# Earlier release of a weight load, transposes split over two PSUM banks, and a ninth Sinkhorn row, in a fused attention and feed-forward kernel

## The chip, the cores and the metric

The kernel runs on one core of a Trainium2 chip. The metric is the device time of one execution in microseconds (us), as a median over several runs. A core has these engines, each with its own instruction queue that is worked off in order: TensorE (PE, matrix products; its weight loads are shown as PEld), VectorE (DVE), ScalarE (ACT), GpSimd (POOL) and SyncE (SP). They synchronize by semaphores. Data moves between the main memory and the on-chip buffer SBUF by DMA, issued here from the queues of POOL and SP. PE writes its products to PSUM[...]; DVE and ACT copy them from there to SBUF.

## The reference

For each of 4 batches and 8 heads, `sort_net` is an 8x8 matrix that is normalized in five Sinkhorn rounds. With it the blocks of k and v are mixed (a sequence of 768 is 8 blocks of 96), then each block of q attends to its block of the mixed k and v. The result, laid out as 3072 tokens of 512, goes through a feed-forward layer.

```
for _ in range(5):
    P = P - np.max(P, axis=-1, keepdims=True)
    P = np.exp(P)
    P = P / (np.sum(P, axis=-1, keepdims=True) + 1e-09)
    P = P / (np.sum(P, axis=-2, keepdims=True) + 1e-09)
k_sorted = einsum('bhij,bhjcd->bhicd', P, k_b); v_sorted likewise
attn = softmax(scale * q_b @ k_sb^T);  x = attn @ v_sb
h = x @ w_in;  g = s * max(h, 0)^2 + b;  out = g @ w_out
```

## The kernel before, in words

The order of the work on each engine is the order in which the program records it (`manual_schedule`); nothing is reordered later. The program is written out by hand in two parts: a start-up for batch 0, and then a steady course in which the feed-forward products of one batch are interleaved with the attention of the next.

**Start-up.** SP loads `sort_net` (L74) and v of batch 0 (L78). POOL builds an identity and a selection matrix, then issues three loads of k (L88) and four of q (L99) of batch 0. Meanwhile the five Sinkhorn rounds run as a chain between ACT (exponential, L190) and DVE: row sums (L195), reciprocal, scaling, column sums (L200), reciprocal, scaling (L205). In the first round the 1e-9 is added to the column sums as an operation of its own (L203), from the tile `eps` (L109). PE has nothing to do in this time and computes products of zeros, `warm(138, 128)` at L188: 138 products of 128 columns into a PSUM tile Z of the pool psb.

After the rounds PE spreads the matrices over the partitions (L217), DVE builds from that the block matrix PD[0] of batch 0 (L235), and PE mixes k with it in three pieces (L254), v in four pieces (L304), with q transposed in between (L273). ACT ("A") and DVE ("D") copy the pieces out of PSUM (`evac`, L243 and L245). Then come the scores of the first half of batch 0 (`s_piece`, L319, exponential on ACT L324), the products with v (`p_piece`, L354) and their normalization on DVE (L361, L362), which gives x.

**POOL's queue and w_in.** After the first loads POOL does three memsets and then a one-element copy that serves as a gate:

```
nc.gpsimd.tensor_copy(out=ones[:, 0:1], in_=KS[0][:, 0, 0, 2 * CK:2 * CK + 1])
load_w()
```

It reads an element that the third k piece's copy (on ACT) writes, so POOL waits there until that is done. `load_w` (L126 to L147) issues the weights of the feed-forward layer: w_in in 16 parts (L131), the second half of batch 0's q in four parts (L99) after the sixth of them, then w_out in four parts (L147). Behind these stand in POOL's queue, in this order: eleven memsets (L496 to L502, L150 to L152), two one-value loads (s and b, L505), k and v of batch 1 (L88), q of batch 1 in eight parts (L99), and eight copies that permute batch 1's v (`v_sort`, L171). POOL's transfers use eight semaphores in turn, so that each issue waits until the transfer eight places earlier has landed.

**The transposes of x.** `t_piece` (L371) turns x with PE into a bank of psb (which has two buffers) and copies it to XT. With "AD", the first half of the bank is copied by ACT and the second by DVE. In the built program the DVE copy waits for the ACT copy of the same bank. With "D", DVE copies the whole. The first call, `t_piece(0, 0, 0, "AD")` at L490, takes heads 0 to 3 of x; the second, as `TP(0, 0, 2, "D")`, heads 4 to 7.

**Feed-forward.** `ffn1(t, slots, ahead)` computes h in eight parts, each a PSUM tile of psa (three buffers) made of 8 products with w_in (L411): for each of two column groups, four products over the four head pairs. With `ahead=3`, the products of head pairs 0 and 1 of parts 0 to 2 come first, and those of head pairs 2 and 3 afterwards. ACT applies the relu (L425), DVE squares (L426). `slots` says which other work is recorded where: a key -3, -2 or -1 stands ahead of part 0, 1 or 2 of these early products. For batch 0:

```
ffn1(0, {-2: [TP(0, 0, 2, "D")], ("pre", 1): [QB(0, HB, "D"), QB(0, HB + 2, "D")],
```

QB are the transposes of the second half of q (L286). `ffn2` computes the products with w_out (L436), each finished group of 128 rows being scaled and biased on DVE (L457) and stored by SP (L460). In its slots lies the attention of the next batch: k pieces (L254) in slot 2, v pieces 0 to 2 (L304), which need the copies of L171, in slot 5, v piece 3 and scores in slot 9.

Of the kernel before, what the change touches and what calls it, by code (L numbers as in the profile page):

```python
# [9 lines left out]
FP = mybir.dt.float32  # L10
BF = mybir.dt.bfloat16
AF = mybir.ActivationFunctionType
ALU = mybir.AluOpType
# [9 lines left out]
def kernel(  # L23
# [12 lines left out]
    nc = tc.nc  # L36

    B, H, S, D = q.shape
    NB = sort_net.shape[-1]
    BLK = S // NB  # L40
    BH = B * H
# [4 lines left out]
    HB = NB // 2  # L46
# [6 lines left out]
    CK = 16  # L53
# [5 lines left out]
    const = ctx.enter_context(tc.tile_pool(name="const", bufs=1))  # L59
# [9 lines left out]
    psb = ctx.enter_context(tc.tile_pool(name="psb", bufs=2, space=bass.MemoryType.PSUM))  # L69
    ctx.enter_context(tc.manual_schedule())  # L70


    sn = const.tile([BH, NB, NB], FP)
    nc.sync.dma_start(out=sn, in_=sort_net.rearrange("b h i j -> (b h) i j"))  # L74
    v0f = gtp.tile([128, C2, D], FP, tag="gt", name="v0f")
    CV = C2 // 4
    for c in range(0, C2, CV):
        nc.sync.dma_start(out=v0f[:, c:c + CV, :].rearrange("p c d -> p (c d)"),  # L78
                          in_=raw[2][0][:, c * D:(c + CV) * D])
# [25 lines left out]
    KS = [const.tile([128, NG, 2, GAP], BF, name=f"ks{i}") for i in range(2)]  # L105
    VS = [const.tile([KR, 2 * NG, VW], BF, name=f"vs{i}") for i in range(2)]
    nc.vector.memset(VP[0][:, :, C2:GAP], 0.0)
    nc.vector.memset(KS[0][:, :, :, C2:GAP], 0.0)
    eps = const.tile([BH, NB], FP)  # L109
    nc.vector.memset(eps, 1e-9)  # L110


    ident = const.tile([128, 128], BF)
# [8 lines left out]
    ones = const.tile([128, 32], BF)  # L122
# [3 lines left out]
    def load_w():  # L126
        wiv = moe_w_in.rearrange("(a p) f -> p a f", p=128)
        fq = d_ff // 4

        def part(a, f0, f1):  # L130
            nc.gpsimd.dma_start(out=wi[:, a, f0 * fq:f1 * fq], in_=wiv[:, a, f0 * fq:f1 * fq])  # L131

        for c in (0, 1):
            for a in (0, 1):
                part(a, c, c + 1)
        for c in (0, 1):
            for a in (2, 3):
                part(a, c, c + 1)
            if c == 0:
                load_q(0, range(HB, NB))  # L140
        for c in (2, 3):
            for a in range(NHP):
                part(a, c, c + 1)
        wov = moe_w_out.rearrange("(f p) n -> p f n", p=128)
        for c in range(4):
            fs = slice(c * (NF // 4), (c + 1) * (NF // 4))
            nc.gpsimd.dma_start(out=wo[:, fs, :], in_=wov[:, fs, :])  # L147
# [9 lines left out]
    def warm(n, w=512):  # L157
        for _ in range(n):
            if not Z:
                Z.append(psb.tile([128, 512], FP, tag="b", name="z"))  # L160
            nc.tensor.matmul(out=Z[0][:, 0:w], lhsT=zeros[:, 0:128], rhs=zeros[:, 0:w],  # L161
                             start=True, stop=True)


    def permute(eng, b, src, cs=slice(0, C2), ds=slice(0, D)):
# [4 lines left out]
        else:  # L170
# [3 lines left out]
    rstat = const.tile([BH, NB], FP)  # L174
# [5 lines left out]
            out=jsel, in_=ident.rearrange("p (h j z) -> p j h z", h=H, j=NB), axis=AX.XY, op=ALU.add),  # L180
        lambda: nc.vector.tensor_reduce(
            out=bm.rearrange("p (e z a) -> p e z a", e=2, z=2),
            in_=idv.rearrange("p a e j z -> p e z a j"), axis=AX.X, op=ALU.add),
# [1 line left out]
    nc.vector.tensor_reduce(out=rstat, in_=sn, axis=AX.X, op=ALU.max)  # L185
    nc.vector.tensor_tensor(out=sn, in0=sn, in1=rstat.broadcast_to([BH, NB, NB]),
                            op=ALU.subtract)
    warm(138, 128)  # L188
    for it in range(5):
        nc.scalar.activation(out=sn, in_=sn, func=AF.Exp)  # L190
        if it >= 1:
            permute(nc.scalar, 0, v0f, slice((it - 1) * CV, it * CV))
        if it in (1, 2):
            idle[it - 1]()
        nc.vector.tensor_reduce(out=rstat, in_=sn, axis=AX.X, op=ALU.add)  # L195
        nc.vector.reciprocal(out=rrec, in_=rstat)
        nc.vector.tensor_tensor(out=sn, in0=sn, in1=rrec.broadcast_to([BH, NB, NB]), op=ALU.mult)
        if it == 4:
            break
        nc.vector.tensor_reduce(out=rstat, in_=sn.rearrange("p i j -> p j i"),  # L200
                                axis=AX.X, op=ALU.add)
        if it == 0:
            nc.vector.tensor_tensor(out=rstat, in0=rstat, in1=eps, op=ALU.add)  # L203
        nc.vector.reciprocal(out=rrec, in_=rstat)
        nc.vector.tensor_tensor(out=sn, in0=sn, in1=spread(rrec, [[0, NB], list(rrec.ap[1])]),  # L205
                                op=ALU.mult)

    PD = {}
# [4 lines left out]
    def spread_p(b0, n):  # L213

        pe = psa.tile([128, n, NB, NB], FP, tag="a", name="pe")
        for b in range(n):
            nc.tensor.matmul(out=pe[:, b].rearrange("p i j -> p (i j)"), lhsT=emat[:, b0 + b, :],  # L217
                             rhs=sn.rearrange("p i j -> p (i j)"), start=True, stop=True)
        return pe
# [13 lines left out]
    def build_pd(b):  # L233
        pd = const.tile([128, 2, 2, NG], BF, name=f"pd{b}")
        nc.vector.scalar_tensor_tensor(  # L235
            out=pd.rearrange("p e z (a i) -> p (e z a) i", i=NB),
            in0=spread(bm, [list(bm.ap[1]), [0, NB]]), scalar=RC[:, b:b + 1],
            in1=spread(PT[:, b], [[0, 4 * NHP], list(PT.ap[2])]), op0=ALU.mult, op1=ALU.mult)
        PD[b] = pd

    def evac(eng, out, in_):
        if eng == "A":
            nc.scalar.copy(out=out, in_=in_)  # L243
        else:
            nc.vector.tensor_copy(out=out, in_=in_)  # L245
# [125 lines left out]
    def t_piece(b, half, hp2, eng):  # L371

        x = X[b, half]
        if hp2 == 0:
            XT[b * 2 + half] = xtp.tile([128, HB, NHP, BLK], BF, tag="xt", name="xt")
        tr = psb.tile([128, 1024], BF, tag="b", name="tr")
        for hp in (hp2, hp2 + 1):
            for n in range(HB):
                c0 = (n * 2 + hp % 2) * BLK
                nc.tensor.transpose(out=tr[:, c0:c0 + BLK],  # L380
                                    in_=x[:, n, hp * 128:(hp + 1) * 128],
                                    identity=ident[0:BLK, 0:BLK])
        n = HB // len(eng)
        for i, g in enumerate(eng):
            evac(g, XT[b * 2 + half][:, i * n:(i + 1) * n, hp2:hp2 + 2, :],
                 tr[:, i * n * 2 * BLK:(i + 1) * n * 2 * BLK].rearrange("p (n a c) -> p n a c",
                                                                        n=n, a=2))

    def t_dma(b, half):
        x = X.pop((b, half))  # L390
# [71 lines left out]

    take_p(0, 1, spread_p(0, 1))
    build_pd(0)
    pe = spread_p(1, B - 1)
    nc.scalar.copy(out=PB, in_=pe)
    warm(3)
    k_piece(0, 0, "A")
    k_piece(0, CK, "D")
    k_piece(0, 2 * CK, "A")  # L470

    nc.gpsimd.tensor_copy(out=ones[:, 0:1], in_=KS[0][:, 0, 0, 2 * CK:2 * CK + 1])
    load_w()
    v_piece(0, 0, "D")
    v_piece(0, CK, "A")
    q_piece(0, 0, "D")
# [66 lines left out]
    def SB(b, h, i): return lambda: s_banks(b, h, i)  # L543
    def P(b, h, i): return lambda: p_piece(b, h, i)
    def TP(b, h, i, eng): return lambda: t_piece(b, h, i, eng)
    def TD(b, h): return lambda: t_dma(b, h)
    def PDB(b): return lambda: build_pd(b)
    def QB(b, n0, eng): return lambda: q_blocks(b, n0, eng)


    ffn1(0, {-2: [TP(0, 0, 2, "D")], ("pre", 1): [QB(0, HB, "D"), QB(0, HB + 2, "D")],
             2: [SB(0, 1, 0)], 3: [SB(0, 1, 1), P(0, 1, 0)], 4: [SB(0, 1, 2), P(0, 1, 1)],
             5: [SB(0, 1, 3), P(0, 1, 2)], 6: [TP(0, 1, 0, "D"), P(0, 1, 3)]}, ahead=3)
    ffn1(1, {-2: [TP(0, 1, 2, "D")], 1: [lambda: take_p(1, B - 1, PB), PDB(1)], 4: [PDB(2)],
# [10 lines left out]
    for b in range(B):  # L565
        n = b + 1
# [48 lines left out]
```

## Time and profile before

| | us |
|---|---|
| median of 8 runs | 231.03 |
| lowest, highest | 229.9, 232.16 |
| the profiled execution, whole | 231.2 |
| its span, first to last instruction | 229.4 |
| PE, PEld busy in the span | 219.3, 132.9 |
| DVE, ACT, POOL busy | 124.5, 98.9, 68.0 |

The chain of work that ended last, which the profile follows back from the last instruction, spends 72% of the span on PE, 14% on DMA, 7% on POOL, 3% on DVE, 1% on ACT. By line, the products with w_out (L436) have 33%, those with w_in (L411) 27%, the DMA of v of a later batch 8% and the DMA of w_in 5%.

How to read the rows: in the timeline and in the chain, the first number is the start in us from the span's start, the second the duration. A group of instructions is written as line, engine, operation, output tile <- input tiles, shape and number; in square brackets stands for how long the engine was idle before it, and what ended that. In a table of stages, each row gives the stretch and its length, the busy time and number of instructions of PE, PEld, DVE, ACT and POOL, then the granted clock of PE, the busy share of the DMA engines and their GB/s. The granted clock is 1.00 throughout.

### The profile page before, as it was taken

Reading aid. Unit: us, or ns where it says so; the run is one execution under the profiler, and the core shown is the slowest. Engines: PE = TensorE matmul, PEld = TensorE weight load, DVE = VectorE, ACT = ScalarE, POOL = GpSimd, SP = SyncE. Lnnn points to the kernel's source line nnn. Section 1 sums busy time; section 2 is a strip of 40 time slices with the busy share of each in tenths; the row PEclk is TensorE's granted clock in tenths of the full one; section 3 lists DMA queues with packets and bytes.
Section 4 is the critical chain, followed back from the end, with each engine's and each line's share of the span. In section 5 each row is a group of like instructions: output and inputs, shape, how many; then the busy total and the mean of one; then the engine's idle time right before and its main releaser. Section 6 shows DMA issues by size and latency. Waiting matters only on the chain.

```text
span 229.4 us, 5829 instructions
## 1 busy us (share of the span) xinstructions
PE 219.3 (96%) x2554; PEld 132.9 (58%) x2554; DVE 124.5 (54%) x224; ACT 98.9 (43%) x127; POOL 68.0 (30%) x112
## 2 busy tenths in 40 slices
PE   8897889999799999999999999999999999999993
PEld 8886546655456555665655555665555555654452
DVE  6666556562456554478647634498647534341221
ACT  4967266564314506554425225637142246650000
POOL 8419789331920007483000009290000000000000
PEclk9999999999999999999999999999999999999999
DMA  6998999999981555995111477994112440001212
GB/s 199 224 64 95 172 184 198 174 186 168 78 209 46 115 122 122 201 155 114 51 46 49 114 163 147 176 168 61 49 68 67 122 114 3 0 1 46 93 49 91
DMA packets 53930, 25.82 MB, mean 113 GB/s; under 512 B 44944, under 2 KB 49296, under 8 KB 53904
## 3 DMA queue, kind: packets, MB, share of 16 engines
q0 software_dynamic: 30864, 12.85, 46.4%
q1 hardware_dynamic: 23040, 12.59, 22.1%
q8 instruction: 20, 0.33, 0.6%
q14 instruction: 6, 0.05, 0.1%
HBM read 27.27 MB, written 6.29 MB: 146 GB/s over the span
## 4 chain that ended last, share of the span: by engine, by line
PE 72%; DMA 14%; POOL 7%; DVE 3%; ACT 1%; issue 1%; POOLq 0%
PE ops L436 33%; PE hps L411 27%; DMA rawv<-in_v_dram 8%; DMA wi<-in_moe_w_in_dram 5%; PE pv L354 3%; PE tv L304 2%; PE sc L319 2%; POOL vp L171 2%; PE tp L254 2%; PE ops L449 2%; POOL wo L147 1%; POOL wi L131 1%; ACT ks L243 1%; DMA sn<-in_sort_net_dram 1%; ACT sn L190 1%
## 5 line engine op out<-in xcount | busy, mean ns | idle before, releaser
L411 PE MATMUL hps<-xt,wi 128*128 128x384 bf16 x512 | 85.7, 326 | 1.8 <-DMA wi<-in_moe_w_in_dram 1.1
L436 PE MATMUL ops<-wo,gt 128*128 128x512 bf16 x368 | 85.7, 379 | 0.0
L425 ACT ACTIVATE rt<-hps 128x768 bf16<-128x768 f32 x64 | 51.1, 811 | 57.3 <-PE hps L411 49.7
L411 PEld LDWEIGHTS <-wi 128*128 128x128 bf16 x512 | 49.4, 98 | 35.0 <-DMA wi<-in_moe_w_in_dram 1.3
L426 DVE TENSOR_TENSOR gt<-rt 128x768 bf16<-128x768 bf16 x64 | 46.5, 733 | 42.5 <-ACT rt L425 41.7
L436 PEld LDWEIGHTS <-gt 128*128 128x128 bf16 x368 | 33.6, 98 | 36.9 <-issue 0.6
L457 DVE SCALAR_TENSOR_TENSOR ot<-ops,s_bc,bias 128x512 f32<-128x512 f32 (+1 forms) x25 | 18.2, 730 | 30.9 <-PE ops L436 28.4
L324 ACT ACTIVATE at<-sc 112x768 bf16<-112x768 f32 x28 | 21.3, 808 | 30.5 <-PE sc L319 30.5
L99 POOL DMA_DIRECT2D qtok<-in_q_dram x32 | 24.9, 792 | 20.5 <-DMA rawv<-in_v_dram 9.0
L362 DVE TENSOR_TENSOR x<-pv,rec 96x512 bf16<-96x512 f32 x32 | 22.0, 687 | 1.1
L245 DVE CAST vs<-tv 112x1024 bf16<-112x1024 f32 x11 | 13.3, 1223 | 11.7 <-PE tv L304 11.6
L171 POOL COPY vp<-rawv 128x384 bf16<-128x384 bf16 x24 | 18.9, 838 | 0.0
L354 PEld LDWEIGHTS <-at 112*128 112x128 bf16 (+1 forms) x256 | 12.8, 101 | 6.7 <-ACT at L324 0.6
L561 POOL COPY gate<-gt 128x1 bf16<-128x1 bf16 x2 | 0.4, 191 | 54.4 <-DVE gt L426 54.4
L354 PE MATMUL pv<-vs,at 112*128 112x66 bf16 (+1 forms) x256 | 13.9, 195 | 0.5 <-DVE vs L245 0.5
L161 PE MATMUL z<-zeros 128*128 128x128 bf16 (+1 forms) x144 | 11.3, 245 | 1.0 <-DVE zeros L102 1.0
L304 PEld LDWEIGHTS <-vp 128*64 128x64 bf16 x512 | 9.3, 112 | 4.6 <-issue 2.7
L304 PE MATMUL tv<-pd,vp 128*64 128x64 bf16 x512 | 10.6, 197 | 1.4 <-POOL vp L171 1.3
L161 PEld LDWEIGHTS <-zeros 128*128 128x128 bf16 x144 | 9.7, 109 | 1.3 <-DVE zeros L102 1.0
L243 ACT CAST ks<-tp 128x1024 bf16<-128x1024 f32 x8 | 8.1, 1012 | 4.4 <-PE tp L254 4.3
L243 ACT CAST vs<-tv 112x1024 bf16<-112x1024 f32 x5 | 5.1, 1018 | 10.3 <-PE tv L304 10.3
L131 POOL DMA_DIRECT2D wi<-in_moe_w_in_dram x16 | 8.6, 548 | 3.1 <-DMA wi<-in_moe_w_in_dram 1.9
(77 smaller groups left out, 104.0 us busy)
## 6 DMA issues: line engine op xcount, KB each, us to landing
out_dram<-ot SPq DMA_DIRECT2D x23, 256.0 KB, 2.0
qtok<-in_q_dram POOLq DMA_DIRECT2D x32, 96.0 KB, 9.4
rawk<-in_k_dram POOLq DMA_DIRECT2D x3, 768.0 KB, 6.5
rawv<-in_v_dram POOLq DMA_DIRECT2D x3, 768.0 KB, 9.8
wi<-in_moe_w_in_dram POOLq DMA_DIRECT2D x16, 128.0 KB, 5.5
wo<-in_moe_w_out_dram POOLq DMA_DIRECT2D x4, 512.0 KB, 10.6
v0f<-in_v_dram SPq DMA_DIRECT2D x4, 384.0 KB, 4.1
rawk<-in_k_dram POOLq DMA_DIRECT2D x3, 256.0 KB, 7.5
```

The source lines that it names most:

```text
L99: nc.gpsimd.dma_start(out=QTOK[b][:, n], in_=qv[:, n])
L161: nc.tensor.matmul(out=Z[0][:, 0:w], lhsT=zeros[:, 0:128], rhs=zeros[:, 0:w], start=True, stop=True)
L171: eng.tensor_copy(out=o, in_=i)
L304: nc.tensor.matmul(out=ps[z * GAP:(z + 1) * GAP, d, :], lhsT=VP[b % 2][:, d0 + d, :], rhs=PD[b][:, :, z, :], start=True, stop=True)
L324: nc.scalar.activation(out=at, in_=sc[0:KR, :, 0:TG], func=AF.Exp, scale=scale)
L354: nc.tensor.matmul(out=pv[0:m, e, n * VW:(n + 1) * VW], lhsT=atf[:, c0:c0 + m], rhs=VS[b % 2][:, e * NG + g0 + n, :], start=True, stop=True)
L362: nc.vector.tensor_tensor(out=x[:, :, hp * 128:(hp + 1) * 128].rearrange("p n (e d) -> p e n d", e=2), in0=pvv[:, :, :, 0:D], in1=rec.unsq ...
L411: nc.tensor.matmul(out=H1[i][:, f, 0:TG], lhsT=wi[:, hp, fc:fc + 128], rhs=xt[:, :, hp, :], start=(hp == 0), stop=(hp == NHP - 1))
L425: nc.scalar.activation(out=rt, in_=h, func=AF.Relu)
L426: nc.vector.tensor_tensor(out=gt[:, 2 * i:2 * i + 2, :], in0=rt, in1=rt, op=ALU.mult)
L436: nc.tensor.matmul(out=ops, lhsT=gt[:, f, m * 128:(m + 1) * 128], rhs=wo[:, f, :], start=(f == 0), stop=(f == NF - 1))
L457: nc.vector.scalar_tensor_tensor(out=ot[:, ns], in0=ops, scalar=s_bc, in1=BIAS[0][:, ns], op0=ALU.mult, op1=ALU.add)
```

## The change

- `eps` and its addition go. The tile of the Sinkhorn matrices gets a ninth row, set to 1e-9 once; the column sums run over nine rows. The 1e-9 is thereby added in each of the four rounds that have column sums.
- The products of zeros ahead of the Sinkhorn rounds are 126 of 140 columns, not 138 of 128.
- The gate copy reads an element of PD[0] (DVE, L235) and stands, with `load_w`, directly behind `build_pd(0)`.
- `t_piece` takes a bank of its own for each engine that copies: with "AD", the transposes of the first two blocks go to one bank and those of the other two to another. In the built program no copy waits for the other engine's copy any more.
- The second transposes of batch 0's first half are recorded one place later (key -1, ahead of part 2) and are copied by ACT and DVE ("AD").

```diff
-    sn = const.tile([BH, NB, NB], FP)
+    sne = const.tile([BH, NB + 1, NB], FP)
+    sn = sne[:, 0:NB, :]
...
-    eps = const.tile([BH, NB], FP)
-    nc.vector.memset(eps, 1e-9)
+    nc.vector.memset(sne[:, NB, :], 1e-9)
...
-    warm(138, 128)
+    warm(126, 140)
...
-        nc.vector.tensor_reduce(out=rstat, in_=sn.rearrange("p i j -> p j i"),
+        nc.vector.tensor_reduce(out=rstat, in_=sne.rearrange("p i j -> p j i"),
                                 axis=AX.X, op=ALU.add)
-        if it == 0:
-            nc.vector.tensor_tensor(out=rstat, in0=rstat, in1=eps, op=ALU.add)
...
-        tr = psb.tile([128, 1024], BF, tag="b", name="tr")
-        for hp in (hp2, hp2 + 1):
-            for n in range(HB):
-                c0 = (n * 2 + hp % 2) * BLK
-                nc.tensor.transpose(out=tr[:, c0:c0 + BLK],
-                                    in_=x[:, n, hp * 128:(hp + 1) * 128],
-                                    identity=ident[0:BLK, 0:BLK])
         n = HB // len(eng)
         for i, g in enumerate(eng):
+            tr = psb.tile([128, 1024], BF, tag="b", name="tr")
+            for hp in (hp2, hp2 + 1):
+                for m in range(n):
+                    c0 = (m * 2 + hp % 2) * BLK
+                    nc.tensor.transpose(out=tr[:, c0:c0 + BLK],
+                                        in_=x[:, i * n + m, hp * 128:(hp + 1) * 128],
+                                        identity=ident[0:BLK, 0:BLK])
             evac(g, XT[b * 2 + half][:, i * n:(i + 1) * n, hp2:hp2 + 2, :],
-                 tr[:, i * n * 2 * BLK:(i + 1) * n * 2 * BLK].rearrange("p (n a c) -> p n a c",
-                                                                        n=n, a=2))
+                 tr[:, 0:n * 2 * BLK].rearrange("p (n a c) -> p n a c", n=n, a=2))
...
     take_p(0, 1, spread_p(0, 1))
     build_pd(0)
+
+    nc.gpsimd.tensor_copy(out=ones[:, 0:1], in_=PD[0][:, 0, 0, 0:1])
+    load_w()
     pe = spread_p(1, B - 1)
...
-    nc.gpsimd.tensor_copy(out=ones[:, 0:1], in_=KS[0][:, 0, 0, 2 * CK:2 * CK + 1])
-    load_w()
     v_piece(0, 0, "D")
...
-    ffn1(0, {-2: [TP(0, 0, 2, "D")], ("pre", 1): [QB(0, HB, "D"), QB(0, HB + 2, "D")],
+    ffn1(0, {-1: [TP(0, 0, 2, "AD")], ("pre", 1): [QB(0, HB, "D"), QB(0, HB + 2, "D")],
```

## The prediction

> **What bounds the kernel now.** I read the slices of the page first: PE is at 9 tenths nearly everywhere, except in the first eight slices (0 to 46 us) and around slice 11. By the stage table PE is busy 15.8 of 20.0 us from 10 to 30, 22.35 of 22.40 from 30 to 52.4, 9.97 of 11.23 from 52.4 to 63.63, and 162.2 of 165.8 from there to the end. So PE sets the time from 63.63 on, and what can be gained or lost lies before. There I read the chain of work that ended last:
>
> ```profile
> 15.82 0.19 POOL ones L472
> 16.01 0.29 issue
> 16.29 1.09 POOL wi L131 x2
> 17.38 5.96 DMA wi<-in_moe_w_in_dram
> ...
> 24.28 5.67 DMA wi<-in_moe_w_in_dram
> ...
> 39.20 18.05 DMA rawv<-in_v_dram
> 57.25 0.28 issue
> 57.54 0.77 POOL qtok L99
> 58.30 0.04 issue
> 58.35 4.80 POOL vp L171 x6
> 63.15 0.04 issue
> 63.19 0.44 PE tv L304 x16
> ```
>
> From 15.82 to 63.19 the chain is not on PE. It is POOL's queue: the gate copy that releases w_in (L472), w_in and w_out, eleven memsets, the loads of batch 1, and the eight copies of batch 1's v (L171) for which PE waits. The links are fixed work: at most eight of POOL's transfers are in flight (each waits for the one eight places earlier), so POOL issues when an old one lands. Nothing between waits for PE. Therefore the whole chain moves with its first link. Next the timeline around that link, and the places where PE waits:
>
> ```profile
> 12.50 0.35 DVE L235 SCALAR_TENSOR_TENSOR pd<-bm,RC,PT 128x128 bf16<-128x128 f32 x1
> ...
> 15.82 0.19 POOL L472 COPY ones<-ks 128x1 bf16<-128x1 bf16 x1 [7.51 <-ACT ks L243]
> ...
> 23.01 0.36 DVE L245 COPY xt<-tr 128x384 bf16<-128x384 bf16 x1 [1.24 <-ACT xt L243]
> ...
> 29.99 0.66 PE L411 MATMUL hps<-xt,wi 128*128 128x384 bf16 x3 [1.09 <-DMA wi<-in_moe_w_in_dram]
> ```
>
> POOL sits idle 7.51 us before the gate copy, while the block matrix was ready at 12.85. The table by quarter microseconds (last column GB/s) tells whether the DMA engines would be free:
>
> ```profile
> 14.25:14.50 0.25, 0.25 (x24) 0.25 (x18) 0.25 (x1) 0.25 (x1) 0.00 (x0) 1.00 0.22 14
> 15.00:15.25 0.25, 0.25 (x25) 0.25 (x20) 0.25 (x1) 0.25 (x1) 0.00 (x0) 1.00 0.00 0
> 17.25:17.50 0.25, 0.25 (x24) 0.25 (x19) 0.25 (x1) 0.00 (x0) 0.25 (x2) 1.00 0.00 0
> ```
>
> They move 150 GB/s until 13.5, 5 to 75 until 15.0, and nothing from 15.0 to 17.5, when w_in's first bytes come, 1.2 us after its first issue at 16.29.
>
> **The change, part by part.**
>
> *The ninth Sinkhorn row.* It removes one 32x8 addition on DVE, on the path: from 4.08 to the next start at 4.27, 0.19 us. The four column sums read 72 elements instead of 64. Their row is 0.260 us; if all of it grew with the elements, 8 more would cost 0.033 each, 0.13 for four; if it is fixed cost, nothing. So the gain lies between 0.06 and 0.19; I take 0.12. The memset of the row takes the place of the memset of eps, and ends before the sort_net transfer lands (2.28).
>
> *126 products of 140 columns.* 17,640 columns for 17,664. The 138 took 9.34 us, so by columns the 126 take 9.33 and by number 8.53; they end between 9.5 and 10.3. The Sinkhorn ends at 11.02 - 0.12 = 10.90, so both are covered by 0.6 us. Nothing.
>
> *The release of w_in.* The gate copy now waits for the block matrix: 12.85 - 0.12, and 0.07 (DVE gt to the gate copy at 87.08) to 0.14 (ACT ks to the gate copy) for the release, so about 12.83 instead of 15.82: 3.0 us earlier. All of load_w and what follows it on POOL is moved past nothing else: behind the gate copy stand the same 16 w_in, four q and four w_out issues, memsets and batch 1's loads in the same order; in front of it the waits for k's and q's old transfers (landed at 13.0 and 15.3 at the latest) are met when POOL reaches them (w_in 4 at 14.9, q 6 at 17.3). ACT's first k copies, which the gate copy used to wait for, lose a reader and nothing else.
> The transfers: w_in's first bytes come at 12.83 + 0.47 + 1.2 = 14.5 instead of 17.5. They meet q's tail for 0.5 us, when it moves under a third of full rate. Cost between 0 and 0.5; I take 0.05, as the tail's bytes are few. So every landing is about 2.95 to 3.0 earlier: the eighth w_in 29.94 to 27.0, rawv 57.25 to 54.3, the sixth v copy 63.15 to 60.2.
>
> A rule of the Trainium skill speaks against this part ("SBUF — State Buffer", Who interferes with whom): DVE and GpSimd share a port pair, and a DVE copy or cast in a two-port mode shuts GpSimd out for its whole length, descriptor writing included. POOL's issues would now lie beside four DVE copies (14.15, 15.44, 16.95, 18.15: 1.23 + 1.23 + 0.96 + 1.23 = 4.65 us). By the full lock, w_in would lose all it gains. The row: before, six w_in issues stood beside the last two of these and took 3.23 us, 0.538 each, the median of all 16, and the cast beside them took 1.23 like those alone. The page itself exempts an instruction with at most one SBUF input outside those modes, and these copies read PSUM. I take the row: no cost.
>
> *The transposes in two banks.* Before, DVE's half of the first copy waits for ACT's half (1.24 us idle, start 23.01 as ACT ends at 22.98): the built program has that wait, and the changed one has not. The second bank is the one that the zero products use, so its transposes wait for the last of them (21.73 + 0.38 = 22.11, before at about 22.13): 0 to 0.1 us. DVE's copy then starts at about 22.45, 0.55 earlier, and so do the two normalizations behind it on DVE (the last ends at 24.5, not 25.04).
>
> *The second transposes one place later, on both engines.* Four products of part 1 now stand before them, in time in which PE waited for the normalization. ACT gets one copy more (0.48), at 24.8 to 25.3, where it idles 4.45 us.
>
> PE's sum at this place: last transposes at 24.5 to 24.8; 12 products at 0.164 (16 of them at 25.27 to 28.04, less the drain) to 26.8; q's transposes 0.84, to 27.6 (q lands at 25.0); four products of part 2, to 28.3 (its w_in has landed at 27.0, so the wait of 1.09 is gone). Before, this ended at 30.65: PE gains 2.3.
>
> **What is late next.** PE reaches batch 1's v at 59.90 - 2.3 = 57.6. Three v pieces at 0.62 (the 32 products of row L304 at 67.19) would end at 59.5, but the sixth v copy is there at 60.2 and the last 16 products end at 63.63 - 3.0 = 60.65. So the wait for POOL remains, shortened from 1.9 (63.63 less 59.90 + 1.87) to 1.1 us, and POOL's chain sets the gain: 3.0 us. PE's own gain only has to be over 1.15 for that, so the transposes' edits and the Sinkhorn's direct part cost and bring nothing by themselves; without this cover the release alone would be worth less. After 60.65 PE goes back to back as before; batch 1's q transposes and gated loads of later batches shift with it.
>
> Sum: the profiled execution took 231.2 around a span of 229.4; less 3.0 it is 228.2 and 226.4. The median of the runs shown is 0.17 under the profiled one, so 228.1.
>
> **Rivals.**
> 1. Part of the shift is lost (chance 0.10). w_in's descriptors and k's and q's tail share the 16 DMA engines, or a landing further down comes later than rigid. The chain's two waits for w_in then lengthen by up to 0.5 each, and PE's gain can fall to 1: 1.0 to 2.0 us remain, 229.0 to 230.1. For it: transfers wait on each other in a chain of eight, so a loss is passed on. Against: 2.5 us without a byte, and no other traffic in the stretch.
> 2. No change (0.07): batch 1's v is held by something that does not move, a DMA backlog that only drains at its rate. From 30 to 44 the engines move about 205 GB/s without pause. Then PE comes earlier and waits longer, 231.0. Against: the backlog begins with w_in, and starts earlier.
> 3. Slower (0.08): the port lock above, in spite of the row. Place: POOL's issues at 13 to 19.5 and the DVE copies there. Price: POOL held for up to 4.65 us less the 3.0 won, so the chain ends 1.6 later, 232.7. It decides from the point at which DVE holds POOL for more than 3.0 us (or a DVE copy, held in turn, delays PE by over 3.4, its gain and the slack). For it, that DVE and POOL now work side by side from 13.3; against, the unchanged 0.538 and 1.23.
>
> Forecast 0.75. A difference under 0.5% (1.2 us) can't be told from none here. Faster: the forecast and most of rival 1, 0.82; within: 0.10; slower: 0.08. Range: the runs spread by 0.5% to each side, their median by less; 227.1 is the gain with a further microsecond (w_in's landings quicker than before), and 230.0 takes in most of rival 1.
>
> **What would show it.** In the changed profile the gate copy stands near 12.8 and w_in's first issue near 13.3, each w_in issue still 0.54; the wait of 1.09 for w_in is gone; DVE's xt copy starts within 0.1 of its transposes; rawv lands near 54.3; PE still waits for vp, about 1.1 in all; the v pieces end near 60.65 and the rest of the span is 165.8 as before. It is wrong if POOL's issues lengthen, if rawv's landing moves by less than 2.5, or if PE has no wait for vp left.

## The result, and the profile after

The changed kernel takes 228.95 us, the median of 18 runs (227.38 to 229.9), against 231.3 of the kernel before, the median of 53 runs. The ratio is 0.9909, with an interval of 0.9889 to 0.9929: 2.1 us of 231.3 are gone (1.6 to 2.6). Ratio and interval leave out the executions of a slower state, of which the kernel before has more, and so the ratio is not simply 228.95 / 231.3. The forecast was 228.1, a gain of 3.0. The profiled execution of the changed kernel took 227.38 around a span of 225.6; it is the shortest of the 18 and 1.57 under their median, so what its rows show is the change at its best.

The first view is the timeline of POOL around the gate and around batch 1's v (start, duration, engine, line, operation, then the idle time before it and what ended that):

```profile
12.87 0.19 POOL L463 COPY ones<-pd 128x1 bf16<-128x1 bf16 x1 [4.56 <-DVE pd L233]
13.35 3.24 POOL L131 DMA_DIRECT2D wi<-in_moe_w_in_dram  x6 [0.29 <-issue]
...
35.67 0.58 POOL L89 DMA_DIRECT2D rawv<-in_v_dram  x1
...
53.19 0.77 POOL L100 DMA_DIRECT2D qtok<-in_q_dram  x1 [2.95 <-DMA rawv<-in_v_dram]
54.00 6.34 POOL L171 COPY vp<-rawv 128x384 bf16<-128x384 bf16 x8
```

The gate copy stands at 12.87, and the six w_in issues beside the DVE copies take 0.54 each, as before. The v copies start at 54.00, where they started at 58.35: 4.35 earlier, though the gate moved by 2.95. The timeline of PE of the same kernel, at the start-up's end and at batch 1's v:

```profile
24.93 2.17 PE L408 MATMUL hps<-xt,wi 128*128 128x384 bf16 x12
26.93 0.84 PE L284 MATMUL tqb<-ident,qtok 96*128 96x96 bf16 x16
27.61 0.82 PE L408 MATMUL hps<-xt,wi 128*128 128x384 bf16 x4
28.41 0.20 PE L332 MATMUL scb<-qt,ks 64*128 64x96 bf16 x1
28.87 0.33 PE L332 MATMUL scb<-qt,ks 64*128 64x96 bf16 x7 [0.26 <-DVE qt L243]
...
58.15 1.71 PE L302 MATMUL tv<-pd,vp 128*64 128x64 bf16 x96
59.78 3.41 PE L433 MATMUL ops<-wo,gt 128*128 128x512 bf16 x15
```

The wait of 1.09 for w_in is gone, and a small one for a q copy has come (28.87). At 58.15 PE runs through its 96 products with v in one group, without a single wait for POOL. In the kernel before it came at 59.90 and waited four times, by the timeline of PE of before:

```profile
59.90 0.69 PE L304 MATMUL tv<-pd,vp 128*64 128x64 bf16 x32
60.85 0.44 PE L304 MATMUL tv<-pd,vp 128*64 128x64 bf16 x16 [0.25 <-POOL vp L171]
...
63.19 0.44 PE L304 MATMUL tv<-pd,vp 128*64 128x64 bf16 x16 [0.33 <-POOL vp L171]
```

In the chain of work of the changed kernel, the line of shares by engine says it in short, where before PE had 72%, DMA 14% and POOL 7%:

```profile
PE 90%; DVE 5%; ACT 2%; issue 1%; DMA 1%
```

POOL is no longer in the chain. The three v pieces end at 58.15 + 1.71 = 59.86, against 63.63, and the rest of the span is 225.6 - 59.86 = 165.7, as before.

### The profile page after: what moved, and what is told of

The parts are those of the page before. It is cut to its first block, busy times and chain, and to the rows that moved or that the text cites. A ratio compares the mean times of both kernels' runs of the same rounds, so it can differ in the third digit from the quotient of the medians.

```text
span 225.6 us, 5806 instructions
## 1 busy us (share of the span) xinstructions
PE 219.0 (97%) x2542; PEld 133.2 (59%) x2542; DVE 124.3 (55%) x223; ACT 99.5 (44%) x128; POOL 68.0 (30%) x112
## 4 chain that ended last, share of the span: by engine, by line
PE 90%; DVE 5%; ACT 2%; issue 1%; DMA 1%
PE ops L433 36%; PE hps L408 36%; PE tv L302 4%; PE pv L352 4%; PE sc L317 3%; PE tp L252 2%; PE ops L446 2%; ACT rt L422 1%; DMA sne<-in_sort_net_dram 1%; ACT sne L190 1%; PE z L161 1%; DVE vs L243 1%; PE tr L380 1%; PE scb L332 1%; DVE rstat L200 1%
## 5 line engine op out<-in xcount | busy, mean ns | idle before, releaser
L423 DVE TENSOR_TENSOR gt<-rt 128x768 bf16<-128x768 bf16 x64 | 46.7, 736 | 41.2 <-ACT rt L422 40.4
L454 DVE SCALAR_TENSOR_TENSOR ot<-ops,s_bc,bias 128x512 f32<-128x512 f32 (+1 forms) x25 | 18.2, 730 | 30.8 <-PE ops L433 28.3
L161 PE MATMUL z<-zeros 128*128 128x140 bf16 (+1 forms) x132 | 11.6, 256 | 1.2 <-DVE zeros L104 1.2
L302 PE MATMUL tv<-pd,vp 128*64 128x64 bf16 x512 | 10.0, 197 | 0.2
```

The lines of the kernel that those rows point to most:

```text
L302: nc.tensor.matmul(out=ps[z * GAP:(z + 1) * GAP, d, :], lhsT=VP[b % 2][:, d0 + d, :], rhs=PD[b][:, :, z, :], start=True, stop=True)
L423: nc.vector.tensor_tensor(out=gt[:, 2 * i:2 * i + 2, :], in0=rt, in1=rt, op=ALU.mult)
L454: nc.vector.scalar_tensor_tensor(out=ot[:, ns], in0=ops, scalar=s_bc, in1=BIAS[0][:, ns], op0=ALU.mult, op1=ALU.add)
```

## The experiments

That last number makes the runs easy to compare. In all fourteen profiles the span less the end of these v pieces is between 165.7 and 165.8 us. So whatever a kernel gains or loses has happened by then, and three columns tell how: when PE arrives at the pieces, when POOL starts its v copies, and whether PE waits for them.

| kernel | ratio to before | interval | median (runs) | PE arrives | v copies start | PE waits for v copies | v pieces end | span |
|---|---|---|---|---|---|---|---|---|
| before | 1 | | 231.3 (53) | 59.90 | 58.35 | four times, 1.26 | 63.63 | 229.4 |
| after | 0.9909 | 0.9889 to 0.9929 | 228.95 (18) | 58.15 | 54.00 | no | 59.86 | 225.6 |
| rel_only | 0.9894 | 0.9863 to 0.9925 | 228.36 (6) | 59.11 | 53.68 | no | 60.82 | 226.6 |
| no_rel | 0.9993 | 0.9965 to 1.0021 | 230.77 (22) | 59.16 | 57.57 | four times, 1.18 | 62.81 | 228.6 |
| tr_only | 0.9993 | 0.9964 to 1.0022 | 231.37 (22) | 59.91 | 57.84 | three times, 0.89 | 63.08 | 228.8 |
| pool_late2 | 0.9901 | 0.9876 to 0.9927 | 228.69 (22) | 59.38 | 54.75 | no | 61.09 | 226.9 |
| after_again | 0.9916 | 0.9887 to 0.9945 | 229.29 (9) | 60.09 | 56.72 | no | 62.03 | 227.8 |
| after_138 | 0.9888 | 0.9842 to 0.9934 | 228.11 (6) | 58.34 | 54.10 | no | 60.05 | 225.8 |
| after_150 | 0.9908 | 0.9878 to 0.9939 | 228.57 (10) | 57.94 | 54.55 | no | 59.81 | 225.6 |
| rel_126 | 0.9967 | 0.994 to 0.9993 | 230.15 (22) | 62.49 | 56.69 | no | 64.20 | 230.0 |
| after_126b | 0.9913 | 0.9882 to 0.9943 | 228.92 (6) | 58.60 | 55.28 | no | 60.53 | 226.3 |
| after_138b | 0.9893 | 0.9865 to 0.992 | 228.45 (6) | 58.52 | 55.80 | once, 0.35 | 61.09 | 226.9 |
| after_114 | 0.9934 | 0.991 to 0.9957 | 229.46 (22) | 61.78 | 54.52 | no | 63.49 | 229.2 |
| best_pre0 | 0.9883 | 0.9846 to 0.9921 | 228.04 (6) | 57.64 | 55.16 | twice, 0.68 | 60.40 | 226.2 |

Each ratio is to runs of the kernel before that were taken beside that run (46, 46 or 27 of them, with medians of 231.15, 231.37 and 231.02). The last five columns are of one profiled execution each. The kernel of "after" is profiled three times: as after, after_again and after_126b it arrives at 58.15, 60.09 and 58.60, so a single profile is no measure of a gain below 2 us.

### Which part carries the gain

My theory after the result was that the release alone moves the time. The rival was that PE's own edits (transposes, Sinkhorn row) do.

**rel_only**: the kernel before with the release of w_in moved, and nothing else.

```diff
     build_pd(0)
+    nc.gpsimd.tensor_copy(out=ones[:, 0:1], in_=PD[0][:, 0, 0, 0:1])
+    load_w()
...
-    nc.gpsimd.tensor_copy(out=ones[:, 0:1], in_=KS[0][:, 0, 0, 2 * CK:2 * CK + 1])
-    load_w()
```

> The kernel before with the earlier release of w_in alone. Recorded theory: 3.0 less 0.12 for the Sinkhorn part is kept, since PE only needs 1.15 of its own gain: ratio 0.9875, the same as the full change within 0.2%. Rival (PE binds after the change): PE gains only the 1.09 us wait for w_in and the v wait of 1.9, so about 0.7 to 1 us less than the full change: ratio 0.993 to 0.995 where the full change has 0.990.

**no_rel**: the changed kernel with these four lines put back where they were, so with the other edits only.

> The changed kernel with the gate copy of w_in put back behind the third k piece; transposes, ninth row and zero products stay as changed. Both theories: the chain on POOL is 0.13 us earlier only (Sinkhorn), PE's gain at the transposes is taken back by w_in's late landing and the wait for batch 1's v: ratio 0.998 to 1.000. If it is under 0.996, the transposes carry the gain and both theories fall.

**tr_only**: the kernel before with the banks of `t_piece` split and the second transposes moved, and nothing else.

```diff
-    ffn1(0, {-2: [TP(0, 0, 2, "D")], ...
+    ffn1(0, {-1: [TP(0, 0, 2, "AD")], ...
```

> The kernel before with the transposes in two banks and the second ones a place later on both engines, nothing else. Recorded theory and rival agree: PE reaches batch 1's v up to 0.9 us earlier and waits there for POOL's copies, ratio 0.998 to 1.002. Under 0.996 would say that the wait for the copies is not what holds the kernel before.

The release alone gives 0.9894, as much as the whole change; all other edits together give 0.9993, and the transposes alone 0.9993. Why the second two bring nothing is seen on PE. In tr_only, DVE's copy of the first transposes starts at 22.62, not 23.01, and part 0's products no longer wait 0.69 for it. But q and w_in, loaded by the old gate, aren't there yet. The timeline of PE of tr_only at that place:

```profile
27.12 0.51 PE L286 MATMUL tqb<-ident,qtok 96*128 96x96 bf16 x8
27.80 0.34 PE L286 MATMUL tqb<-ident,qtok 96*128 96x96 bf16 x4 [0.18 <-DMA qtok<-in_q_dram]
28.46 0.34 PE L286 MATMUL tqb<-ident,qtok 96*128 96x96 bf16 x4 [0.31 <-DMA qtok<-in_q_dram]
29.54 1.14 PE L410 MATMUL hps<-xt,wi 128*128 128x384 bf16 x4 [0.73 <-DMA wi<-in_moe_w_in_dram]
30.60 0.34 PE L334 MATMUL scb<-qt,ks 64*128 64x96 bf16 x8
```

The three DMA waits in brackets eat what the earlier copies had won: the scores of L334 start at 30.60, before at 30.58. And in no_rel, where PE does arrive 0.74 earlier at batch 1's v, it waits there, by the timeline of PE of no_rel:

```profile
59.16 0.69 PE L302 MATMUL tv<-pd,vp 128*64 128x64 bf16 x32
60.02 0.44 PE L302 MATMUL tv<-pd,vp 128*64 128x64 bf16 x16 [0.16 <-POOL vp L171]
60.81 0.44 PE L302 MATMUL tv<-pd,vp 128*64 128x64 bf16 x16 [0.35 <-POOL vp L171]
```

Both of PE's waits that the release removes hang on POOL's queue. The rival falls. The recorded expectation for rel_only had two values: its interval takes in the 0.9875 that went with POOL's chain as the limit, and leaves out the 0.993 to 0.995 that went with PE. But its profile has no wait for POOL, which the first needed:

```profile
59.11 1.71 PE L304 MATMUL tv<-pd,vp 128*64 128x64 bf16 x96
```

**after_again**: the changed kernel once more, beside these.

> The changed kernel once more, for a second profile and a ratio on this chip. The recorded theory (POOL's chain is rigid and sets the gain): ratio 0.987, the sixth v copy of batch 1 ready 3.0 us earlier than in the kernel before, PE still waiting for it by about 1.1 us. The rival (PE's own start-up gain sets it, the chain having run ahead): ratio about 0.990, no wait for the v copies, v pieces reached about 1.8 to 2.3 us earlier.

The ratio repeats (0.9916). Its profile does not: the span is 227.8, the v pieces end 2.17 later than in the first profile of the same kernel, and PE stands still in the middle of a group that waits for no semaphore. The timeline of PE of after_again, in the v pieces of batch 0:

```profile
17.32 0.79 PE L302 MATMUL tv<-pd,vp 128*64 128x64 bf16 x38
19.50 0.60 PE L302 MATMUL tv<-pd,vp 128*64 128x64 bf16 x26 [1.39 <-issue]
20.03 0.52 PE L317 MATMUL sc<-qt,ks 64*128 64x96 bf16 x16
21.51 0.43 PE L352 MATMUL pv<-vs,at 112*128 112x66 bf16 x8 [0.97 <-DVE vs L243]
```

The releaser in the bracket is "issue": nothing that the profile shows was waited for. Rel_only's 64 products run in one group of 1.20 us; in the first profile of the changed kernel the same group took 1.44. The stop is not the whole delay: the v pieces of batch 0 begin at 15.18 here and at 14.58 there, and of these 0.60 some 0.5 come from the zero products, as is told below. This opened the third question below.

### Is POOL's chain rigid?

The prediction had POOL's v copies follow the gate by a fixed distance. They moved by 4.35 for 2.95. Rival: batch 1's v lands when the backlog of transfers ahead of it is through, wherever POOL issued it.

**pool_late2**: the changed kernel with two more zero-fills of the same strip on POOL, ahead of batch 1's loads. They repeat a fill that already stands there.

```diff
     nc.gpsimd.memset(VP[1][:, :, C2:GAP], 0.0)
+    nc.gpsimd.memset(VP[1][:, :, C2:GAP], 0.0)
+    nc.gpsimd.memset(VP[1][:, :, C2:GAP], 0.0)
```

> The changed kernel with two more memsets of 0.96 us on POOL ahead of the loads of batch 1 (they write zeros over zeros). Recorded theory (the chain is rigid and binds): batch 1's v lands 1.9 us later and the time is 1.9 us longer, ratio to before 0.995. Rival 1 (PE binds, the chain has slack of about 0.8): 1.1 longer at most. Rival 2 (the v load lands when the DMA backlog ahead of it has drained, whenever it is issued): landing moves by under 0.5 us and the time by less, ratio as that of the full change.

The timeline of POOL of pool_late2:

```profile
33.46 0.96 POOL L499 MEMSET vp<- 128x1024 bf16 x1
34.47 0.95 POOL L500 MEMSET vp<- 128x1024 bf16 x1
...
38.70 0.54 POOL L89 DMA_DIRECT2D rawv<-in_v_dram  x1
...
53.93 0.77 POOL L100 DMA_DIRECT2D qtok<-in_q_dram  x1 [2.98 <-DMA rawv<-in_v_dram]
54.75 6.33 POOL L171 COPY vp<-rawv 128x384 bf16<-128x384 bf16 x8
```

Batch 1's v is issued at 38.70, 3.03 later than in the changed kernel (2.0 by the fills, the rest because POOL was late before) and only 0.5 earlier than in the kernel before (39.20). Yet the copies start only 0.75 later than in the changed kernel, and 3.6 earlier than before. Against after_again, where v is issued at 37.57, they even start 1.97 earlier after an issue that is 1.13 later. Over all fourteen profiles the copies follow the issue of v by 16.05 (pool_late2) to 19.15 us, so that distance is not fixed, and "rigid" is disproved at this link. The time agrees: 0.9901 (0.9876 to 0.9927), where a rigid chain was expected to give 0.995. What sets the landing is not settled, and the rival of the backlog is not shown by one profile: in the eleven profiles with the early release the copies start between 53.68 and 56.72, kernels with the same POOL program (after 54.00, after_again 56.72) among them. The cause of that spread of 3 us between executions stays open. Either way PE arrives 2.5 to 7.3 us after that start (before: 1.55), so it rarely waits.

### The products of zeros

Their time was to be hidden by the Sinkhorn rounds, 0.6 us to spare. It is not always so. The timelines of PE at the start, of before first and of after_again second:

```profile
1.00 9.34 PE L161 MATMUL z<-zeros 128*128 128x128 bf16 x138 [1.00 <-DVE zeros L102]
11.15 1.07 PE L217 MATMUL pe<-sn,emat 32*128 32x64 f32 x8 [0.82 <-DVE sn L197]
```

```profile
1.21 10.46 PE L161 MATMUL z<-zeros 128*128 128x140 bf16 x126 [1.21 <-DVE zeros L104]
11.60 1.10 PE L215 MATMUL pe<-sne,emat 32*128 32x64 f32 x8
```

In before PE stands idle for 0.82 after them; in after_again the products run until 11.67, and the next work on PE has no wait for DVE. It starts 0.5 us later than the last scaling of the rounds would let it, in pool_late2 0.4. The number of products is not the cause: in rel_126 (126) and rel_only (138) they end alike, at 11.15 and 11.16. In every trace they start at half their later rate (4 or 5 in half a microsecond, then 8 or 9 with 126 or 138), and the step is where the trace's first record of the granted clock (1.00) begins: 4.09 in before, 5.04 in after, 6.75 in after_again, 3.98 to 6.75 in all. So the clock column's 1.00 says nothing of the time ahead of that record, and the products end between 10.28 and 11.67, late in an execution where the full rate comes late.

The second finding concerns their number.

The stop in after_again came after 38 products with their weight loads. The trace records, besides the data, the packets with which PE's own instructions are fetched: a queue named "instruction" moved one packet of 16,384 bytes in that stretch. The DMA queues of after_again from 17 to 18 us (packets, MB, share of 16 engines):

```profile
q0 software_dynamic: 102, 0.09, 82.7%
q8 instruction: 1, 0.02, 6.6%
```

The one instruction packet was under way from 17.09 for 1.05 us, in between POOL's weight and q traffic; PE resumed at 19.50, 1.36 after its end. Theory: 126 products instead of 138 mean 24 fewer instructions (a load and a product each) ahead of this place, so the same block boundary falls later in the program, where w_in now moves early. If so the stop must move by 12 pairs for 12 products, and need both the shorter count and the early release. Rival: the count means nothing, and the stop is an accident of one execution.

**after_138** and **after_150**: the changed kernel with the old count, and with twelve more.

```diff
-    warm(126, 140)
+    warm(138, 128)
```

and `warm(150, 118)`.

> The changed kernel with 138 zero products of 128 columns instead of 126 of 140: the same columns, 24 more PE instructions ahead of the k pieces. New theory (a block of PE's instructions is fetched by DMA; with 24 instructions fewer PE asks for it later, when w_in's transfers already fill the engines, and stands still in the v pieces for 0.16 to 1.5 us until it comes): no gap within the v pieces of batch 0, the fetch starts by 15.0, time 0.2 to 1.4 us shorter than the changed kernel, ratio to before 0.985 to 0.989. Rival (the gap is chance, w_in's release alone makes it): the gap is there as often as in the changed kernel, ratio 0.990 to 0.992.

> The changed kernel with 150 zero products of 118 columns (17,700 columns, 48 PE instructions more than with 126). By the theory of the instruction block: asked for still earlier, no gap, the same time as with 138 within 0.2%, ratio 0.985 to 0.989. By the rival, no difference from the changed kernel: 0.990 to 0.992.

**rel_126**: rel_only with `warm(126, 140)`, so the release and the new count without the other edits.

> The kernel before with the earlier release and 126 products of 140 columns, nothing else. By the theory of the instruction block the gap now shows up in the v pieces without any of the other edits: 0.2 to 1.4 us longer than the release alone (ratio 0.9894), so 0.990 to 0.995. By the rival: as the release alone, 0.989.

**after_126b, after_138b, after_114**: the changed kernel unchanged, with the old count, and with `warm(114, 155)`, side by side on one chip.

> The changed kernel once more, beside its twin with 138 products on the same chip. Theory of the instruction block: a gap of 0.16 to 1.5 us within the v pieces of batch 0, ratio 0.990 to 0.992.

> The changed kernel with 138 products of 128 columns, beside the changed kernel on the same chip. Theory of the instruction block: no gap, 0.5 to 1.2 us shorter than the changed kernel. Rival (the gap costs nothing in the end, since PE waits for batch 1's v anyway): the same time.

> The changed kernel with 114 products of 155 columns (17,670 columns), another 24 PE instructions fewer. By the theory the block boundary lies 12 weight load and product pairs further into the v pieces (after some 50 of the 64, not 38), the block is asked for 0.3 us later still, and the gap is there again, 0.2 to 1.5 us; ratio 0.990 to 0.993. If the gap stays after 38 products, or is gone, the theory falls.

From all fourteen traces, times in us. The pause is the longest time from the start of one product to that of the next in the second 64 products, less the usual 0.03; the idle time in the brackets of the rows is 0.2 shorter, as the product ahead of the pause is shown as still running:

| zero products | w_in released | kernel | instruction packet: start, duration | pause of PE in batch 0's v pieces |
|---|---|---|---|---|
| 138 | late | before | 14.61, 1.27 | 0.04, after 26 products |
| 138 | late | tr_only | 14.78, 1.28 | 0.13, after 26 |
| 126 | late | no_rel | 15.26, 0.95 | none |
| 150 | early | after_150 | 14.27, 1.12 | none |
| 138 | early | rel_only | 14.76, 0.96 | none |
| 138 | early | after_138 | 14.69, 1.53 | 0.26, after 26 |
| 138 | early | after_138b | 14.82, 1.44 | 0.39, after 26 |
| 138 | early | best_pre0 | 14.62, 0.91 | none |
| 126 | early | after | 15.33, 0.95 | 0.21, after 38 |
| 126 | early | after_126b | 15.69, 0.94 | 0.54, after 38 |
| 126 | early | pool_late2 | 16.34, 0.88 | 0.85, after 38 |
| 126 | early | after_again | 17.09, 1.05 | 1.56, after 38 |
| 126 | early | rel_126 | 17.50, 0.96 | 1.52, after 38 |
| 114 | early | after_114 | 16.53, 0.93 | 1.35, after 50 |

The timelines of PE at that group, of after_138b first and of after_114 second:

```profile
16.91 0.60 PE L302 MATMUL tv<-pd,vp 128*64 128x64 bf16 x26
17.73 0.79 PE L302 MATMUL tv<-pd,vp 128*64 128x64 bf16 x38 [0.23 <-issue]
```

```profile
16.79 0.98 PE L302 MATMUL tv<-pd,vp 128*64 128x64 bf16 x50
18.95 0.41 PE L302 MATMUL tv<-pd,vp 128*64 128x64 bf16 x14 [1.18 <-issue]
```

The pause stands after 26, 38 and 50 products for 138, 126 and 114, exactly twelve apart, and in every trace that has one it stands behind the same number of PE's records, 704 or 705. In the nine profiles with a pause of over 0.1 PE goes on 1.27 to 1.55 us after the packet ended (after_again: 17.09 + 1.05 = 18.14, and 19.50). So it is the block of instructions that is late. The place doesn't vary by execution, how late the block comes does, and there the rival stays half right.

Both conditions count: 126 with the late release doesn't pause, 138 and more with the early one by none to 0.39, fewer with the early one by 0.21 to 1.56. The ranges touch, so the length of a single pause proves nothing. What is late is told by the packets. Counted from the first v product of batch 0, the packet starts at -0.30 with 150 products, between -0.10 and 0.08 with 138 and at 0.29 with 126 in no_rel; with 126 and the early release it starts at 0.75 to 1.95, and then takes its usual 0.88 to 1.05. It is thus held up ahead of its start (with 138 and the early release, two of four packets took longer instead, 1.44 and 1.53). That w_in's traffic is what holds it follows from the pair of conditions and is not shown directly. The Trainium skill ("Runtime: NRT & Kernel Launch", Instruction fetch mechanics) says that an engine's sequencer fetches its instructions in 16 KiB blocks over a DMA queue of its own, and that crossing a boundary is mostly hidden. The size agrees with the packet of 16,384 bytes; that it is hidden holds within 0.13 us without w_in's early traffic here, and not beside it.

In time: rel_126 (0.994 to 0.9993) and rel_only (0.9863 to 0.9925) don't overlap; twelve fewer products, each a little wider, cost 0.7%, 1.7 us. Inside the changed kernel the intervals overlap: 0.9888 and 0.9893 with 138, 0.9908 with 150, 0.9909 to 0.9916 with 126, 0.9934 with 114. The expectation for 150 was missed: it has no pause in its profile, and its ratio lies in the range that the rival had. rel_126 (expected at 0.990 to 0.995) and after_114 (0.990 to 0.993) came out longer than expected. About 0.2% (0.5 us) of the change's own ratio may be this cost, less than the runs can prove. Why the packet starts at 15.3 in one execution and at 17.1 in another stays open.

Two profiles show a second cost behind a stop. The stages of rel_126 (stretch, length, busy time of PE, PEld, DVE, ACT and POOL, granted clock, DMA share, GB/s):

```profile
22.00:23.00 1.00, 1.00 (x23) 0.76 (x21) 0.66 (x2) 0.67 (x2) 0.56 (x1) 0.87 2.10 170
23.00:24.00 1.00, 1.00 (x15) 0.63 (x13) 0.82 (x3) 0.56 (x2) 0.84 (x2) 0.50 2.30 156
...
25.00:26.00 1.00, 1.00 (x15) 0.98 (x14) 0.00 (x0) 0.10 (x1) 0.53 (x1) 0.50 1.48 172
26.00:27.00 1.00, 0.48 (x8) 0.32 (x6) 0.56 (x3) 0.38 (x1) 0.08 (x1) 0.93 1.17 104
```

The column after POOL's is the granted clock. A mean of 0.87 is 0.26 us at half clock, 0.93 is 0.14, and three whole rows lie between: 3.4 us at half. So rel_126's profiled span is longer than before's, together with the pause and with Sinkhorn rounds that ended 0.8 late in that execution. In after_114 the clock fell as well, for 6.8 us from 21.9; in after_again, with the same stops, it stayed at 1.00. A mean granted clock is on record for each of these executions, and for 119 of the kernel before: a mean of 0.993 or less, as these falls make, stands in none of the 34 executions with the early release and 138 or 150 products, in 29 of 99 with the early release and fewer, and in 48 of 163 with the late release. So among kernels with the early release the fall goes with the pause, but the kernel before has it too (32 of 119), and no trace shows where in the execution it falls there. In rel_126 it is the smaller part: its 14 executions with a mean of 0.998 or more have a median of 229.84, still 1.5 above rel_only.

### A better version

**best_pre0**: after_138 with q's second-half transposes recorded one part earlier, so that DVE's copies of them stand ahead of the first squares.

```diff
-             ("pre", 1): [QB(0, HB, "D"), QB(0, HB + 2, "D")],
+             ("pre", 0): [QB(0, HB, "D"), QB(0, HB + 2, "D")],
```

> The changed kernel with 138 products of 128, and with the transposes of q's second half recorded one part earlier, so that DVE copies them ahead of the first squares. If PE now binds (the theory), the wait of 0.27 for DVE and the restart beside it go, 0.45 us shorter than with 138 alone, ratio 0.985 to 0.987. If POOL's chain binds (the recorded theory), no difference from 138 alone.

The wait at the scores is gone, and PE arrives at batch 1's v at 57.64, the earliest of all. It then waits again for POOL, by the timeline of PE of best_pre0:

```profile
28.25 0.34 PE L332 MATMUL scb<-qt,ks 64*128 64x96 bf16 x8
...
57.64 1.20 PE L302 MATMUL tv<-pd,vp 128*64 128x64 bf16 x64
59.18 0.44 PE L302 MATMUL tv<-pd,vp 128*64 128x64 bf16 x16 [0.34 <-POOL vp L171]
59.96 0.44 PE L302 MATMUL tv<-pd,vp 128*64 128x64 bf16 x16 [0.34 <-POOL vp L171]
```

With 0.9883 it has the lowest ratio of all, 2.7 us under before, but it can't be told from after_138b beside it (0.9893) or from the changed kernel. PE's gain is met by POOL's copies, which in this execution started at 55.16.

## Why the prediction was right, and which steps were wrong

**The release carries the gain: right.** Shown by rel_only (0.9894) against no_rel and tr_only (0.9993 both).

**The links up to the loads: right.** Gate copy 12.87 (said 12.83), first w_in issue 13.35 (13.3), DVE's first copy of x 22.58 (22.45), last product of part 2 ending at 27.61 + 0.82 = 28.43 (28.3). For the ninth Sinkhorn row, the block matrix starts at 12.37 instead of 12.50, 0.13 (said 0.12); but that agreement is not shown to be more than chance, as the last scaling of the rounds (L197) starts at 10.65 to 11.06 in the ten profiles with the ninth row and at 10.79 to 11.64 in the four without.

**The port lock: absent.** The six w_in issues beside DVE's copies took 3.24 us, 0.54 each. The row decided rightly, as the page's own exemption has it, and rival 3 is out. Rival 2, v held by something that doesn't move, is out as well: v came earlier in every kernel with the release.

**"Therefore the whole chain moves with its first link": wrong.** The v copies came 4.35 earlier, not 3.0, and pool_late2 delayed an issue by 3.03 and the copies by 0.75. I had read "fixed work" out of a chain whose longest piece is a transfer of 18.05 us, in one execution; the spread of 3 us between executions is as large as the shift that I computed.

**"So the wait for POOL remains, ... and POOL's chain sets the gain: 3.0 us": wrong.** No wait for POOL is left in the three profiles of the changed kernel. The one sentence that I had written as the sign of error, "if PE has no wait for vp left", came true. PE itself sets the gain. In the profiled execution the wait and spacing of 1.86 at the v pieces goes (63.63 less 59.90 + 1.87), and PE arrives 59.90 - 58.15 = 1.75 earlier; the sum is 3.6, the span fell by 3.8. In after_again PE arrives 0.19 later, and 1.86 - 0.19 = 1.7 against 1.6 measured. So "the transposes' edits ... bring nothing by themselves" held as they stand alone (0.9993), but beside the release PE's own microseconds count again: after_126b arrives 1.3 earlier, and 3.1 is what its span lost. By time this is seen once: rel_126 (0.994 to 0.9993) has the release and the 126 products, and with the remaining edits it becomes 0.9909 (0.9889 to 0.9929), though the pause weighs on rel_126 in an unknown share. That PE sets the gain is thus shown by the profiles, and by the times only in part. With 138 products rel_only (0.9894) is not told from after_138 (0.9888).

**"PE reaches batch 1's v at 57.6": 0.55 off, by a wait I did not cost.** Up to 28.43 PE was as early as said. Then the scores of the second half wait for DVE's copies of q. The chain of work of the changed kernel at that place (start, duration, engine, what, line):

```profile
26.48 0.82 ACT rt L422
27.30 0.02 issue
27.32 0.56 DVE gt L423
27.88 0.94 DVE qt L243 x2
28.83 0.04 issue
28.87 0.33 PE scb L332 x7
```

DVE's queue has the first squares (L423) ahead of the q copies, and they wait for ACT's relu. Before, PE stood waiting for w_in in this time and the order cost nothing. I had asked what is late next only at batch 1's v, and not at the next product.

**"126 products of 140 columns: Nothing": wrong.** "They end between 9.5 and 10.3" took the mean rate of one execution; with 126 they ended at 10.83 to 11.67, twice (pool_late2, after_again) too late for the rounds to hide them. With 138 they ended at 10.28 to 11.26 and were covered. That is a matter of when the full rate came; what belongs to the number is another cost. I had priced the products as work only. They are also instructions, and 24 fewer move the boundary of a fetched block. Price: pauses of 0.21 to 1.56 us in the profiles, 0.7% between rel_126 and rel_only.

**The size.** Forecast 3.0, measured 2.1 by the ratio. The best profile lost 3.8, the other two of the same program 1.6 and 3.1. That the number came so near is in part luck: POOL's chain, which was to set the gain, moved further than computed, and PE, which was to have time to spare, set it instead. The gain measured is just above rival 1's 1.0 to 2.0. Its place was near, early w_in transfers that share the DMA engines with other traffic, but what came late was PE's instructions, not k's and q's tails. The whole of the missing 0.9 is not accounted for: the old count gives back perhaps 0.5 of it, and the rest is under what the intervals tell apart.

## What to carry to other kernels

When a long wait is removed, walk the next instructions of the freed engine one by one and ask of each what it waits for, as the next cover is often gone a microsecond later. A distance between a DMA's issue and its landing, read from one profile, is not a fixed link once a backlog stands ahead of it: take a second profile of the same program before adding such distances up. Filler instructions aren't free because their time is hidden, and in some executions it isn't: their number decides where an instruction block ends, and an idle gap marked "issue" inside a group without waits is the sign to look at the instruction queue.

## What the runs showed of the hardware

- PE paused 0.21 to 1.56 us inside a run of matmuls when the 16,384-byte packet with its next instructions had to start beside the early w_in traffic; it went on 1.27 to 1.55 us after the packet's end.
- At the start of an execution PE's products ran at half their later rate until 3.98 to 6.75 us, by execution, and the trace has its first record of the granted clock, 1.00, at that moment.
- The granted clock fell to 0.50 for 3.4 us in rel_126, and for 6.8 in after_114, after idle times of at most 1.36 us each (in rel_126 1.36 and 0.97 between 18.5 and 21.85). The Trainium skill ("TensorE: Matmul & The Clock Gate", What's actually happening) has the clock at half after an idle window of about 3.4 us, windows that run freely. The length agrees with rel_126, and twice it with after_114; the idle time needed was less here, and that after_again escaped with the same gaps fits windows that run freely without showing it.
